# Storing a bias tile partition-major, clearing a dispatch buffer only in the general path, and moving 18 column-sum matmuls, in an FFT + MoE + FFN kernel

## The chip, the cores and the metric

The kernel runs on one core of a Trainium2 chip. The metric is the device time of one execution in microseconds, as the median of several runs. Before the change it is 990.84 us (3 runs, 988.04 to 993.03).

## What is computed

Three steps follow each other; the input x is [8, 3072, 256], and all is float32 at the borders.

```python
X = np.fft.fft(np.fft.fft(x, axis=1), axis=2).real     # 8 batches, 3072 x 256
x = X.reshape(24576, 256)                              # tokens
logits = x @ w_gate                                    # 8 experts
e = argmax(logits); gate = softmax(logits)[e]
# first come, first served: each expert takes its first 768 tokens, by token number
h = relu(disp @ w1[e])                                 # 256 -> 1024
out[token] = gate * (h @ w2[e])                        # 1024 -> 256; zero for tokens without a slot
h = out @ w_in                                         # 256 -> 2048
result = (h * sigmoid(1.702 * h)) @ w_out              # 2048 -> 256, [24576, 256]
```

A token without a slot has a zero row in the result. With 8 experts of 768 slots there are 6,144 slots for 24,576 tokens, so once all experts are full, later tokens are zero rows.

## The kernel before, in words

**Main path and general path.** Because slots are given in token order, the kernel transforms and routes only as many tokens as will fill all experts unless the routing is lopsided: five half batches of 1,536 tokens (`nu` = 5, so `nb` = 3 batches). A flag says at the end whether every expert was filled. If not, `tc.If(more != 0)` at the end of the program enters the general path, which transforms the other batches and repeats the FFNs. With these inputs it isn't entered.

**The transform.** A batch comes as three thirds (row tiles j) of 1 MB, each loaded by SP (`fft_x`, L434) into one of three buffers. `fft_fold` (L444 ff.) adds and subtracts parts on DVE, and the tile is then split into a rounded part (`fhi`, on ACT, L346) and the rest (`flo`, on DVE, L347). For j = 2 the fold also sends two small pieces across partitions by DMA (L468, L469), and ACT copies two more (L470, L471). The first batch takes its thirds in the order 0, 1, 2, the others 0, 2, 1.

The **S stage** (`fft_s`, matmuls of L520) multiplies the folded thirds by cosine and sine tables (`chi`, `clo`) into PSUM tiles `psP`, `psPE`, `psQ` and so on; the third tile ends them. `fft_s_full` (L575 to L592) turns them into `hiP` and `hiQ` in SBUF, on ACT and DVE. The **D stage** (`fft_d`, matmuls of L603 and L607) multiplies these by a second table (`dr`, `dhi`) and gives, in 12 token tiles, the rows of two half batches with their gate logits, copied into `xtok`. The folds of the next batch stand between the D stage's tiles.

**The column sums.** `fft_rows` (L410 ff.) makes one piece for all batches at once: 18 matmuls (L423) into two PSUM tiles `pt` of 8 rows, two conversions on ACT (L425), and a split into `trh` (ACT) and `trl` (DVE). The last matmuls of each batch's S stage into `psQ` take `trh` and `trl` (`sel` picks the batch). It also stores the `bias` tile, 128 x 6 x 8 float32, to `biasd` in DRAM (L414), which only the general path reads. A hook in the S stage of the first batch calls it: `(i, n) == (1, 0)`, that is with the first piece of the second row tile.

**Routing.** For each half batch `choose` and `route` (L647 to L713) find each token's expert on DVE, count with small matmuls, and give each token a slot (`sloti`) or an index out of bounds. POOL then sends the rows to `disp` in DRAM by 12 indirect DMAs per half batch (L713), 128 rows of 260 floats each. `disp` has 6,144 rows; `zero_disp` clears it by eight stores of 768 rows from SP (L263), called at three places: one store behind the small constants' loads, two between loads of x ahead of the first S stage's end, five after it. `self.after(ins, self.last_load)` keeps each behind the load of x issued last.

**The FFNs.** After the third half batch the first blocks of three experts are read back by POOL (`xr`, L841, which waits for the scatters' landing), scaled by the gate (L853) and transposed on PE (L871). The expert FFN goes in blocks of up to three tiles of 128 slots (L898 and L889); the second FFN runs six blocks behind (L943 and L934), and its rows go to `out` by indirect DMA (L965) with the token numbers `ix` (L857). SP stores zero rows to `out` beside it (L271).

**Order of the work.** Each engine, and the SP queue of DMA issues, works through one list in order. The lists come from the order of the calls and from a scheduler; `self.after` pins single pairs.

Of the kernel before, what the change touches and what calls it, by code (L numbers as in the profile page):

```python
# [22 lines left out]
P = 128  # L23
# [15 lines left out]
TINY = float(np.uint32(0x38100000).view(np.float32))   # upper word of 2 ** -126  # L39
XB = 3          # thirds of a batch on chip  # L40
XR = 3          # blocks of rows loaded ahead
SB = 3          # slot tiles per block of the FFN
FIRST = 3       # experts whose first blocks come before all others
ZC = 6          # parts of a half batch's zero rows
LAG = 6         # blocks that the second FFN runs behind the first
D1 = 3          # hidden tiles that the second product of an FFN runs behind the first
# row tiles of the first batch in the order of their loads, and of the others
J0, J1 = (0, 1, 2), (0, 2, 1)
# when a batch's row tiles are folded, during the batch before: "s" at the end of its S stage, "n" with the
# S stage of their own batch, a number with that token tile of the D stage  # L50
FOLD = ((0, "s", 6), (0, 8, 11))
DEXACT = (0, 1)   # batches whose D stage takes float32 operands as they are
SPLIT = (1,)      # batches whose first half is routed in two parts
CHOOSE, ROUTE = 6, 10   # token tiles of the D stage after which the first part is chosen for and routed
EARLY = 9         # token tile of the last D stage after which the first block is turned
LATE = 5          # hidden tile of the first block from which on the last half batch is routed
IN0, IN1 = 5, 7   # hidden tiles with which the next block is gated and turned
LOADS = 4         # hidden tile with which a later block's rows are read
PACE = (1, 1, 1, 2, 1, 1, 1, 2)   # steps of the second FFN's weights with each hidden tile


# s of an octant by row tile: even, odd, half of each
# [7 lines left out]
def consts():  # L70
    """Tables that depend on the shapes alone."""
# [11 lines left out]
    # high and (scaled) low parts of 11 bits each  # L83
    cm = np.stack(blocks, 1).reshape(NJ, P, NS, 2 * HC)
    # the last tile's odd classes: cosines and sines of even s, sines and cosines of odd s
# [3 lines left out]
    # the even classes' second halves mirror their first ones  # L89
# [3 lines left out]
    cm = np.ascontiguousarray(np.stack([ch, cl], 3))           # [NJ, 2, 128, 2, 4 * HC]  # L93
# [11 lines left out]
    cs = np.stack([C, Sf, Sm], 0).astype(np.float32)          # [3, 128, 256]  # L105
    # mirrored logits backwards, 3 of padding, the row, its start again, 3 of padding, logits
# [3 lines left out]
    # [l in tile, l tile, 3, d]  # L110
# [8 lines left out]
    ], 1).astype(np.float16)                                   # [128, 4, 128]  # L119
# [7 lines left out]
    # the mirrored half's last tile starts with its first token  # L127
# [8 lines left out]
def layout(x):  # L136
    """x as the octants of s that the folds pair, d beside -d."""
    s = ROWS
    rows = [s, 768 - s, 1536 - s, 768 + s, 3072 - s, 2304 + s, 1536 + s, 2304 - s]
    pos = np.arange(128)  # L140
    neg = (256 - pos) % 256
    neg[0] = 128
    p2, n2 = neg.copy(), pos.copy()
    p2[0], n2[0] = 0, 128
    xo = np.empty((B, NJ, P, 8, 2, P), np.float32)
    for i, r in enumerate(rows):
        v = x[:, r, :].reshape(B, NJ, P, D)
        xo[:, :, :, i, 0] = v[..., pos if i < 4 else p2]
        xo[:, :, :, i, 1] = v[..., neg if i < 4 else n2]
    er = x[:, [0, 768, 1536, 2304], :]  # L150
    xe = np.stack([er[..., pos], er[..., neg]], 2)             # [B, 4, 2, 128]
    xed = np.ascontiguousarray(xe.transpose(3, 0, 1, 2))       # [128, B, 4, 2]
    xeb = np.ascontiguousarray(xe[..., 0])                     # [B, 4, 2]
    # columns d = 0 and 128 of all batches: [p, j, half, octant, b]
    xt = np.ascontiguousarray(xo[..., 0].transpose(2, 1, 4, 3, 0))
    return xo, xed, xeb.reshape(B, 8), xt


def at(ap, i):
    """Entry i of the first axis, i a number or a register's value."""  # L160
# [6 lines left out]
class K:  # L167
    def __init__(self, ctx, tc, cap, x, xed, xeb, xt, cm, dc, dct, tri, sel, sm, wg, w1, w2, wi, wo, out):
        self.ctx, self.tc, self.nc = ctx, tc, tc.nc
        self.cap = cap  # L170
        self.capt = -(-cap // P)                  # slot tiles per expert
# [10 lines left out]
    # ---------------------------------------------------------------- setup  # L182
    def setup(self):
# [16 lines left out]
        self.base0 = c0.tile([P, E], F32, name="base0")  # L200
# [11 lines left out]
    def tokens(self, n, extra=None):  # L212
        """Room for the rows of n half batches, used in turn."""
# [7 lines left out]
    def scratch(self, *shape):  # L221
        """A part of that room, until the rows need it."""
# [7 lines left out]
    def small_consts(self):  # L230
# [3 lines left out]
        # the next slot of each expert, at first that where its slots start  # L234
# [5 lines left out]
        nc.gpsimd.tensor_copy(out=self.base0, in_=self.start)  # L240

    def check_full(self, n):
        """Multiplies the flag by: every expert has n tokens or more."""
# [7 lines left out]
    def after(self, ins, first):  # L251
        """Keeps ins behind first, if any, on their queue."""
# [5 lines left out]
    def zero_disp(self, es):  # L258
        nc = self.nc
        for e in es:  # L260
            n = self.capt
            v = self.disp[e * n * P : (e + 1) * n * P].rearrange("(p n) w -> p n w", n=n)
            ins = nc.sync.dma_start(out=v, in_=self.zt[:, None, :].to_broadcast([P, n, ROW]))  # L263
            self.after(ins, self.last_load)

    def zero_out(self, h, i):
        """Rows of a part of half a batch."""
# [5 lines left out]
    # ---------------------------------------------------------------- FFT  # L273
    def fft_consts_alloc(self):
# [6 lines left out]
        # signs of the last tile's even and odd s: cosines and sines, high and low  # L281
# [7 lines left out]
    def fft_consts(self, j, low):  # L289
        """Tables of a row tile: the even classes' columns m as stored and, with the sign of s, from the end."""  # L290
# [26 lines left out]
    def fft_dconsts(self):  # L317
        nc = self.nc
        fc = self.fc
        # D stage tables with the gate's columns  # L320
# [9 lines left out]
    def fft_dtables(self):  # L330
        """The D stage's tables, the gate's columns from their product."""
# [17 lines left out]
    def fft_prelude(self):  # L349
        """Edge rows of all batches, and the even classes of column d = 128 (less d = 0)."""  # L350
# [4 lines left out]
        # sums and differences of d and -d  # L355
# [5 lines left out]
        bias = fc.tile([P, 6, B], F32, name="bias")   # P0, P2, P odd, Q odd, the same with signs, 0  # L361
# [11 lines left out]
        self.biasd = self.dram.tile([B, P, 6], F32, name=f"biasd{self.runs}")  # L373
        self.bias = bias
        self.runs += 1
        # column 128: even classes
# [15 lines left out]
        # row 0 changes sign last in the third class  # L392
# [17 lines left out]
    def fft_rows(self):  # L410
        """The even classes of column d = 128, all batches."""
        nc, fc, fx = self.nc, self.fc, self.fx
        hi, lo, bb = self.pre
        nc.sync.dma_start(out=self.biasd.rearrange("b p i -> p i b"), in_=self.bias)  # L414
# [15 lines left out]
    def fft_x(self, b, j):  # L430
        """A third of a batch."""
# [8 lines left out]
    def fft_fold(self, x, j):  # L440
        """Folds a third of a batch: stationary operands of the S stage."""
# [7 lines left out]
        # x: ee1 ee2 v1 v2 | u1 u2 w1 w2 | P0 Q2 P2 Q0  # L449
# [6 lines left out]
        # column 0 of v carries the cosine transform of d = 128 (odd k)  # L456
# [5 lines left out]
        if j < 2:  # L462
            # v1 v2 u1 u2 | P0 Q2 P2 Q0
            src = x[:, 2:14].rearrange("p (g q) d -> p g q d", q=6)[:, :, 0:4]
        else:
            # P0 Q2 P2 Q0 | v2 v1 and u1 u2 of even s, v1 v2 and u2 u1 of odd s, one below the other
# [11 lines left out]
    def terms(self, half, j):  # L478
        """(chunk, [(data, table)]): even classes, sums over even and over odd s of the odd classes."""
# [9 lines left out]
    def fft_s_begin(self, b):  # L489
        """The S stage, transposed: cosine and sine halves [d', k]. Row 0 of the sine half: d = 128."""  # L490
# [33 lines left out]
    def fft_s_end(self, bias, b=None):  # L524
        """High and low parts of the halves."""
# [12 lines left out]
        # classes 1 and 3 (from its end) as sum and difference  # L538
# [29 lines left out]
    def fft_s_full(self, bias):  # L568
        """The halves as they are."""
# [26 lines left out]
    def fft_row(self, PQ, k0, n, name):  # L596
        """Token rows k0 to k0 + n - 1, in the D stage's columns."""
# [14 lines left out]
    def fft_d(self, PQ, xs, hook=lambda t: None):  # L612
        """Token rows of the first half of a batch and those of the second, with their logits.

        Row S - k is row k backwards. The second half's tiles are in falling order, and so are their
        rows; in place of token S the last tile starts with token S / 2."""
# [13 lines left out]
    # ---------------------------------------------------------------- routing  # L630
    def rt(self, name, n, e=1, dt=F32, swap=False, bufs=1):
        """A tile for n tiles of tokens, or [expert, tile] of them."""
# [5 lines left out]
    def choose(self, xt):  # L638
        """Experts of some tiles of tokens."""
# [9 lines left out]
        # the first of equal maxima  # L649
# [322 lines left out]
def kernel(ctx, tc, cap, x, xed, xeb, xt, cm, dc, dct, tri, sel, sm, wg, w1, w2, wi, wo, out):  # L972
# [56 lines left out]
    def route_next(late=False):  # L1029
# [5 lines left out]
        if u + 1 == nu // 2 * 2:  # L1035
            nc.vector.tensor_copy(out=k.base0, in_=k.base)
# [272 lines left out]
```

## Time and profile before

| what | value |
|---|---|
| median of 3 runs | 990.84 us (988.04 to 993.03) |
| span of the profiled execution | 1001.3 us |
| PE busy | 922.4 us, 92% |
| DVE busy | 592.0 us, 59% |
| ACT busy | 513.4 us, 51% |
| POOL busy | 210.2 us, 21% |
| DMA | 96.71 MB in 78,118 packets, 12,633 of them under 512 bytes |

The profiled execution gives no other time than its span, which is 10.5 us above the median of the runs. PE is TensorE's matmuls, PEld its weight loads, which overlap; DVE is VectorE, ACT ScalarE, POOL GpSimd, and SP (SPq) the queue from which most DMAs are issued. A share of the whole span is a mean over stages with different limits. The granted clock is TensorE's, as a share of full speed. A line number is that of the listing above.

### The profile page before, as it was taken

To read this page: it belongs to the slowest core of one execution; us is meant where nothing else is said; L and a number is where in the kernel's file an instruction comes from. 1 tells how busy PE (TensorE), PEld (TensorE's weight loads), DVE (VectorE), ACT (ScalarE), POOL (GpSimd) and SP (SyncE) were. 2 spreads that over 40 slices of the span, in tenths; PEclk is the share of its full clock that TensorE was granted. 3 is DMA by queue.
4 is the path that set the end of the run, shared out by engine and by line. 5 is a ranking of instruction groups with operands and counts; after the bars stand their busy time and mean duration, and the time that the engine had idled before them with its cause. 6 is when DMAs were issued, how large, how long until landed. Compare 5 with 4: busy or idle time off the path is not lost. (4 is left out here: it accounts for less than half of the span.)

```text
span 1001.3 us, 15819 instructions
## 1 busy us (share of the span) xinstructions
PE 922.4 (92%) x5920; PEld 898.5 (90%) x5920; DVE 592.0 (59%) x1175; ACT 513.4 (51%) x1064; POOL 210.2 (21%) x236
## 2 busy tenths in 40 slices
PE   3779287899989999999999999999999999999995
PEld 2558286889989999999999999999999999999995
DVE  7369185898898456545553555555535555555552
ACT  5546063665675446444553555555535554555452
POOL 4006653755556101010101010101010110111011
PEclk9979698999999999999999999999999999999998
DMA  9996357797781106200530020201000000000000
GB/s 342 34 272 212 138 171 250 249 319 230 251 267 53 33 1 202 83 32 2 173 112 33 1 84 18 78 23 59 1 16 1 17 16 1 17 17 17 1 18 19
DMA packets 78118, 96.71 MB, mean 97 GB/s; under 512 B 12633, under 2 KB 67130, under 8 KB 76880
## 3 DMA queue, kind: packets, MB, share of 16 engines
q1 hardware_dynamic: 71056, 76.53, 26.4%
q0 software_dynamic: 6976, 19.09, 5.5%
q8 instruction: 48, 0.79, 0.3%
q14 instruction: 38, 0.31, 0.1%
HBM read 50.93 MB, written 45.86 MB: 97 GB/s over the span
## 5 line engine op out<-in xcount | busy, mean ns | idle before, releaser
L948 DVE TENSOR_TENSOR sg<-ph,sg 128x384 f32<-128x384 f32 x256 | 142.6, 557 | 116.0 <-ACT sg L947 112.6
L952 DVE TENSOR_TENSOR gl<-sg,gh 128x384 fp32r<-128x384 f32 x256 | 146.1, 571 | 107.9 <-ACT gh L951 105.5
L951 ACT CAST gh<-sg 128x384 fp32r<-128x384 f32 x256 | 131.1, 512 | 121.7 <-DVE sg L948 121.7
L947 ACT ACTIVATE sg<-ph 128x384 f32<-128x384 f32 x256 | 125.8, 491 | 108.0 <-PE ph L943 103.7
L965 POOL DMA_INDIRECT out<-orow,ix x48 | 47.1, 980 | 569.0 <-ACT orow L964 559.3
L904 DVE SCALAR_TENSOR_TENSOR hl<-ph,hh 128x384 fp32r<-128x384 f32 x128 | 70.9, 554 | 92.1 <-ACT hh L903 78.3
L903 ACT ACTIVATE hh<-ph 128x384 fp32r<-128x384 f32 x128 | 63.0, 494 | 90.7 <-PE ph L898 85.5
L889 PE MATMUL py<-hh,w2h 128*128 128x384 f32 x256 | 88.2, 345 | 3.0 <-ACT hh L903 1.9
L889 PE MATMUL py<-hl,w2h 128*128 128x384 f32 x256 | 87.1, 340 | 1.1 <-DVE hl L904 1.0
L898 PE MATMUL ph<-xhi,w1l 128*128 128x384 f32 x256 | 85.9, 336 | 1.7 <-issue 1.7
L889 PE MATMUL py<-hh,w2l 128*128 128x384 f32 x256 | 86.4, 337 | 0.0
L898 PE MATMUL ph<-xhi,w1h 128*128 128x384 f32 x256 | 86.0, 336 | 0.4 <-issue 0.4
L898 PE MATMUL ph<-xlo,w1h 128*128 128x384 f32 x256 | 85.8, 336 | 0.4 <-issue 0.4
L713 POOL DMA_INDIRECT disp<-xtok,sloti x48 | 53.8, 1120 | 66.3 <-DMA x<-in_x 38.2
L889 PEld LDWEIGHTS py<-hh,w2h 128*128 128x128 f32 x256 | 48.7, 190 | 4.1 <-ACT hh L903 2.4
L347 DVE TENSOR_TENSOR w2l<-wraw,w2h 128x512 fp32r<-128x512 f32 x44 | 42.0, 961 | 15.9 <-ACT w2h L346 15.3
L889 PEld LDWEIGHTS py<-hl,w2h 128*128 128x128 f32 x256 | 48.6, 190 | 3.2 <-DVE hl L904 2.5
L898 PEld LDWEIGHTS ph<-xlo,w1h 128*128 128x128 f32 x256 | 48.2, 189 | 1.4 <-issue 1.2
L898 PEld LDWEIGHTS ph<-xhi,w1h 128*128 128x128 f32 x256 | 48.2, 188 | 1.2 <-issue 1.2
L889 PEld LDWEIGHTS py<-hh,w2l 128*128 128x128 f32 x256 | 48.7, 190 | 0.0
L898 PEld LDWEIGHTS ph<-xhi,w1l 128*128 128x128 f32 x256 | 48.2, 188 | 0.5 <-issue 0.5
L347 DVE TENSOR_TENSOR w1l<-wraw,w1h 128x512 fp32r<-128x512 f32 x44 | 31.8, 722 | 2.8 <-ACT w1h L346 1.9
(380 smaller groups left out, 2697.0 us busy)
## 6 DMA issues: line engine op xcount, KB each, us to landing
out<-zt SPq DMA_DIRECT2D x96, 256.0 KB
wraw<-in_w SPq DMA_DIRECT2D x88, 256.0 KB
x<-in_x SPq DMA_DIRECT2D x9, 1024.0 KB
disp<-zt SPq DMA_DIRECT2D x8, 780.0 KB
xr<-disp POOLq DMA_DIRECT2D x16, 390.0 KB
wraw<-in_wi SPq DMA_DIRECT2D x8, 512.0 KB
wraw<-in_wo SPq DMA_DIRECT2D x8, 512.0 KB
cr<-in_cm SPq DMA_DIRECT2D x6, 388.0 KB
```

Source lines behind the costliest of these rows:

```text
L347: return h, nc.vector.tensor_tensor(out=lo, in0=src, in1=hi.bitcast(F32), op=ALU.subtract)
L713: ins = nc.gpsimd.indirect_dma_start(out=self.disp, out_offset=bass.IndirectOffsetOnAxis(ap=sloti[:, i : i + 1], axis=0), in_=xt[:, i, 0:R ...
L889: nc.tensor.matmul(py[a][:, :n], lhsT=w2[f // 2][v][:, f % 2, a * P : (a + 1) * P], rhs=(hh, hl)[u][:, :n], start=(f == 0 and k == 0), sto ...
L898: nc.tensor.matmul(ph[:, :n], lhsT=w1[f // 2][v][:, a, (f % 2) * P : (f % 2 + 1) * P], rhs=(xh, xl)[u][:, a, :n], start=(k == 0), stop=(k ...
L903: self.last_a = nc.scalar.activation(out=hh[:, :n], in_=ph[:, :n], func=AF.Relu)
L904: self.last_v = nc.vector.scalar_tensor_tensor(out=hl[:, :n], in0=ph[:, :n], scalar=0.0, in1=hh[:, :n].bitcast(F32), op0=ALU.max, op1=ALU. ...
L947: nc.scalar.activation(out=sg[:, :n], in_=ph[:, :n], func=AF.Sigmoid, scale=1.702)
L948: nc.vector.tensor_tensor(out=sg[:, :n], in0=ph[:, :n], in1=sg[:, :n], op=ALU.mult)
L951: nc.scalar.copy(out=gh[:, :n], in_=sg[:, :n])
L952: nc.vector.tensor_tensor(out=gl[:, :n], in0=sg[:, :n], in1=gh[:, :n].bitcast(F32), op=ALU.subtract)
L965: ins = nc.gpsimd.indirect_dma_start(out=out, out_offset=bass.IndirectOffsetOnAxis(ap=xr[:, i : i + 1], axis=0), in_=orow, in_offset=None, ...
```

## The change

1. The `bias` tile is stored as it lies in SBUF: `biasd` is [P, 6, B] in place of [B, P, 6]. The general path reads a batch's part from it by a strided load.
2. `zero_disp` loses its three calls in the main path and clears all of `disp` at the start of the general path. That path then begins anew, from batch 0 and from `self.start`, and clears `out` too; so the copy `base0` of the counts goes. Rows of `disp` that no token reached now hold what the memory held, so `ix` is cut off at an index out of bounds.
3. The hook for `fft_rows` moves from `(1, 0)` to `(2, 0)`: from the first piece of the second row tile to the first piece of the third.

The changed file has three lines less ahead of these places, so L414 there is L411, and so on.

```diff
-        self.biasd = self.dram.tile([B, P, 6], F32, name=f"biasd{self.runs}")
+        self.biasd = self.dram.tile([P, 6, B], F32, name=f"biasd{self.runs}")
...
-        nc.sync.dma_start(out=self.biasd.rearrange("b p i -> p i b"), in_=self.bias)
+        nc.sync.dma_start(out=self.biasd, in_=self.bias)
...
-        nc.gpsimd.tensor_copy(out=self.base0, in_=self.start)
...
-    def zero_disp(self, es):
+    def zero_disp(self):
         nc = self.nc
-        for e in es:
+        for e in range(E):
             n = self.capt
             v = self.disp[e * n * P : (e + 1) * n * P].rearrange("(p n) w -> p n w", n=n)
-            ins = nc.sync.dma_start(out=v, in_=self.zt[:, None, :].to_broadcast([P, n, ROW]))
-            self.after(ins, self.last_load)
+            nc.sync.dma_start(out=v, in_=self.zt[:, None, :].to_broadcast([P, n, ROW]))
...
-        ins = nc.vector.tensor_copy(out=ix[:, :ns], in_=xr.bitcast(I32)[:, :ns, 257])
+        ins = nc.vector.tensor_scalar(out=ix.bitcast(U32)[:, :ns], in0=xr.bitcast(U32)[:, :ns, 257], scalar1=OOB,
+                                      scalar2=None, op0=ALU.min)
...
     k.small_consts()
-    k.zero_disp(range(1))
     fold(0, J0[2])
...
-        if u + 1 == nu // 2 * 2:
-            nc.vector.tensor_copy(out=k.base0, in_=k.base)
...
-                if b == 0 and (i, n) == (1, 0):
+                if b == 0 and (i, n) == (2, 0):
                     k.fft_rows()
...
             xload()
-            k.zero_disp(range(1, 3))
             xload()
...
         if b == 0:
-            k.zero_disp(range(3, E))
             xload()
...
     with tc.If(more != 0):
-        nb = nu // 2
...
+        k.zero_disp()
+        for h in range(2 * B):
+            for i in range(ZC):
+                k.zero_out(h, i)
+        nc.sync.dma_start(out=k.smt, in_=k.sm)
...
-                nc.vector.tensor_copy(out=k.base, in_=k.base0)
-                with tc.For_i(nb, B, 1) as b:
+            nc.vector.tensor_copy(out=k.base, in_=k.start)
+            with tc.For_i(0, B, 1) as b:
...
-                    nc.sync.dma_start(out=bt, in_=at(k.biasd, b))
+                nc.sync.dma_start(out=bt[:, :, None], in_=k.biasd[:, :, bass.ds(b, 1)])
```

How the lists move is shown at three places. The first is the SP queue from the load of the table `tri` to the loads of x for the second batch. L263 are the stores that zero `disp`, L414 the bias store, L434 the loads of x. Before:

```order
L233 DMA tri<-in_tri 128x512
L263 DMA disp<-zt 768x1x260
L468 DMA x<-x 64x2x128
L469 DMA x<-x 64x2x128
L494 DMA sf<-in_sel 8x128
L414 DMA biasd_193<-bias 768x8x1
L434 DMA x<-in_x 128x2048
L263 DMA disp<-zt 768x1x260 x2
L434 DMA x<-in_x 128x2048
L263 DMA disp<-zt 768x1x260
L468 DMA x<-x 64x2x128
L469 DMA x<-x 64x2x128
```

and now (three lines less, so L411 is the bias store and L431 a load of x):

```order
L232 DMA tri<-in_tri 128x512
L465 DMA x<-x 64x2x128
L466 DMA x<-x 64x2x128
L491 DMA sf<-in_sel 8x128
L411 DMA biasd_192<-bias 128x48
L431 DMA x<-in_x 128x2048 x2
L491 DMA sf<-in_sel 8x128 x2
L465 DMA x<-x 64x2x128
L466 DMA x<-x 64x2x128
L431 DMA x<-in_x 128x2048 x3
```

The zeroing stores are gone, and loads of x stand next to each other behind the bias store.

The second place is ACT, at the end of the first batch's S stage: L425 are the two conversions of the column sums, `fhi` of L346 is the third row tile's rounded part. Before:

```order
L471 COPY x<-x 64x256
L425 ACTIVATE xtokx<-pt_301,bb 8x386
L425 ACTIVATE xtokx<-pt_312,bb 8x384
L346 CAST trh<-xtokx 8x772
L346 CAST fhi<-x 128x1024
L496 CAST sel_267<-sf 8x128
L592 ACTIVATE hiP<-psP_269,bias 128x386
```

and now, with L422 the conversions and L343 the cast:

```order
L468 COPY x<-x 64x256
L343 CAST fhi<-x 128x1024
L493 CAST sel_264<-sf 8x128
L589 ACTIVATE hiP<-psP_266,bias 128x386
L589 ACTIVATE hiP<-psP_270,bias 128x384
L335 COPY dr<-pw 128x2x8
L336 COPY dr<-pw 128x2x8
L343 CAST dhi<-dr 128x560
L422 ACTIVATE xtokx<-pt_337,bb 8x386
L422 ACTIVATE xtokx<-pt_348,bb 8x384
L577 ACTIVATE eb<-psPE,bias 128x384
L343 CAST trh<-xtokx 8x772
```

The conversions stood ahead of the third tile's cast; they now follow `hiP`'s two rows, and the cast of `trh` is the last of these.

The third is DVE at the same place: `trl` is the rest of the column sums, L444 the first add of a fold (of the next batch's thirds), L581 to L587 make `hiP` and `hiQ`. Before:

```order
L347 TENSOR_TENSOR trl<-xtokx,trh 8x772
L347 TENSOR_TENSOR flo<-x,fhi 128x1024
L581 TENSOR_TENSOR hiP<-eb,psPO 128x384
L583 TENSOR_TENSOR hiP<-eb,psPO 128x384
L444 TENSOR_TENSOR x<-x 128x1024
L347 TENSOR_TENSOR dlo<-dr,dhi 128x560
L581 TENSOR_TENSOR hiQ<-eb,psQO 128x384
L587 SCALAR_TENSOR_TENSOR hiQ<-psQO,ngs,t_411 128x384
```

and now (L441 is the first add of a fold):

```order
L344 TENSOR_TENSOR flo<-x,fhi 128x1024
L441 TENSOR_TENSOR x<-x 128x1024
L344 TENSOR_TENSOR dlo<-dr,dhi 128x560
L443 TENSOR_TENSOR x<-x 128x512
L444 TENSOR_TENSOR x<-x 128x512
L448 TENSOR_TENSOR x<-x 128x512
L449 TENSOR_TENSOR x<-x 128x512
L441 TENSOR_TENSOR x<-x 128x1024
L344 TENSOR_TENSOR trl<-xtokx,trh 8x772
L578 TENSOR_TENSOR hiP<-eb,psPO 128x384
L580 TENSOR_TENSOR hiP<-eb,psPO 128x384
L578 TENSOR_TENSOR hiQ<-eb,psQO 128x384
```

One fold's start stood ahead of `hiQ`; now two (a whole first fold but for its split, and the first add of the second) stand ahead of `trl`, `hiP` and `hiQ`.

## Rows read from the trace of the kernel before

**Rows 1.** Part 1 of the page: the span.
```profile
span 1001.3 us, 15819 instructions
```

**Rows 2.** Busy us by stretch: length, PE, PEld, DVE, ACT, POOL; clock, DMA, GB/s.
```profile
100.00:125.00 25.00, 6.96 (x30) 5.82 (x28) 4.37 (x26) 1.23 (x4) 17.09 (x20) 0.62 0.39 138
...
200.00:225.00 25.00, 23.81 (x134) 22.47 (x134) 24.51 (x41) 15.77 (x32) 14.27 (x12) 1.00 0.98 319
...
700.00:800.00 100.00, 100.00 (x683) 100.00 (x682) 51.38 (x95) 49.48 (x103) 5.83 (x6) 1.00 0.02 9
```

**Rows 3.** Who waited for whom, 0 to 235 us: total, times, longest.
```profile
POOL disp L713 <- DMA x<-in_x: 38.2, 1, 38.2
...
DVE x L444 <- DMA x<-in_x: 23.7, 3, 15.0
```

**Rows 4.** Timeline of the SP queue: start, duration of the issue, what.
```profile
26.42 0.60 SPq L414 DMA_DIRECT2D biasd<-bias  x1
27.12 9.19 SPq L434 DMA_DIRECT2D x<-in_x  x1
```

**Rows 5.** Busy time by stretch, 32 to 36 us.
```profile
32.00:36.00 4.00, 4.00 (x23) 3.55 (x21) 2.17 (x2) 2.26 (x4) 0.00 (x0) 1.00 1.92 1
```

**Rows 6.** Timeline of DVE: start, duration, what, idle time before and its releaser.
```profile
5.88 1.23 DVE L444 TENSOR_TENSOR x<-x 128x1024 f32<-128x1024 f32 x1 [4.86 <-DMA x<-in_x]
...
53.34 1.22 DVE L444 TENSOR_TENSOR x<-x 128x1024 f32<-128x1024 f32 x1 [15.04 <-DMA x<-in_x]
...
63.86 1.23 DVE L444 TENSOR_TENSOR x<-x 128x1024 f32<-128x1024 f32 x1 [3.80 <-DMA x<-in_x]
...
76.07 0.17 DVE L699 SCALAR_TENSOR_TENSOR sloti<-over,pos 128x12 int32<-128x12 f32 x1
```

**Rows 7.** Timeline of PE, at the changes of stage.
```profile
24.20 0.49 PE L423 MATMUL pt<-chi,thi 128*8 128x386 f32 x1 [4.25 <-ACT thi L346]
...
41.38 0.63 PE L603 MATMUL pe<-dr,hiP 128*1 128x280 f32 x2
...
56.74 2.23 PE L603 MATMUL pd<-dr,hiQ 128*128 128x280 f32 x4 [13.12 <-DVE hiQ L587]
...
69.36 0.55 PE L520 MATMUL psP<-chi,fhi 128*128 128x386 f32 x1
...
97.97 0.54 PE L520 MATMUL psP<-chi,fhi 128*128 128x386 f32 x1
...
135.83 0.96 PE L607 MATMUL pd<-dhi,hiP 128*128 128x280 f32 x5
...
145.72 0.95 PE L871 MATMUL pt<-smt,xr 128*128 128x128 f32 x6
...
148.06 0.34 PE L898 MATMUL ph<-xhi,w1h 128*128 128x384 f32 x1
```

**Rows 8.** Timeline of POOL: scatters and the first reads of blocks.
```profile
80.59 1.23 POOL L713 DMA_INDIRECT disp<-xtok,sloti  x1 [38.21 <-DMA x<-in_x]
...
97.16 1.12 POOL L713 DMA_INDIRECT disp<-xtok,sloti  x1 [0.23 <-issue]
...
120.78 0.97 POOL L713 DMA_INDIRECT disp<-xtok,sloti  x1 [0.23 <-issue]
...
138.54 2.34 POOL L841 DMA_DIRECT2D xr<-disp  x3 [1.83 <-DMA disp<-xtok,sloti]
```

**Rows 9.** Busy time of line 423 alone, 19 to 32 us.
```profile
19.00:32.00 13.00, 4.68 (x18) 1.80 (x18) 0.87 0.72 158
```

**Rows 10.** Timeline of ACT: two rows of the first batch, one of the third.
```profile
29.44 0.40 ACT L471 COPY x<-x 64x256 f32<-64x256 f32 x1
...
32.45 1.04 ACT L346 CAST fhi<-x 128x1024 fp32r<-128x1024 f32 x1
...
124.77 0.58 ACT L535 ACTIVATE eb<-psPE,bias 128x384 f32<-128x384 f32 x1 [20.99 <-remote]
```

**Rows 11.** Busy time of line 603 alone, 85 to 98 us.
```profile
85.00:98.00 13.00, 12.42 (x52) 9.21 (x52) 1.00 0.36 124
```

More of the change, by code (lines that the diff above doesn't have):

```diff
@@ L199, in setup @@
         self.base = c0.tile([P, E], F32, name="base")
-        self.base0 = c0.tile([P, E], F32, name="base0")
         self.flag = c0.tile([P, 1], F32, name="flag")
@@ L1236 @@
     with tc.If(more != 0):
-        nb = nu // 2
-        if nb < B:
-            with ExitStack() as c1:
-                k.rp = c1.enter_context(tc.tile_pool(name="rp2", bufs=1))
-                k.fxt = c1.enter_context(tc.tile_pool(name="fxt2", bufs=1))
-                k.tokens(2)
-                k.fq = c1.enter_context(tc.tile_pool(name="fq2", bufs=1))
-                k.fc = c1.enter_context(tc.tile_pool(name="fc2", bufs=1))
-                k.fx = c1.enter_context(tc.tile_pool(name="fx2", bufs=2))
-                k.fft_consts_alloc()
-                for j in range(NJ):
-                    k.fft_consts(j, nc.vector)
-                k.fft_dconsts()
-                k.fft_dtables()
-                k.fft_prelude()
-                k.fft_rows()
-                nc.vector.tensor_copy(out=k.base, in_=k.base0)
-                with tc.For_i(nb, B, 1) as b:
-                    data = {j: k.fft_load(b, j) for j in J1}
-                    bt = k.fx.tile([P, 6], F32, name="bt", tag="bt", bufs=1)
-                    nc.sync.dma_start(out=bt, in_=at(k.biasd, b))
-                    k.fft_s_begin(b)
-                    for j in J1:
-                        k.fft_s(b, j, data[j])
-                    PQ = k.fft_s_end(bt)
-                    xs = [next(k.slot) for _ in range(2)]
-                    k.fft_d(PQ, xs)
-                    for mir, xt in enumerate(xs):
-                        k.route(xt, mir, None)
@@ new lines @@
+        k.zero_disp()
[3 more added lines that the diff above has]
+        nc.sync.dma_start(out=k.smt, in_=k.sm)
+        with ExitStack() as c1:
+            k.rp = c1.enter_context(tc.tile_pool(name="rp2", bufs=1))
+            k.fxt = c1.enter_context(tc.tile_pool(name="fxt2", bufs=1))
+            k.tokens(2)
+            k.fq = c1.enter_context(tc.tile_pool(name="fq2", bufs=1))
+            k.fc = c1.enter_context(tc.tile_pool(name="fc2", bufs=1))
+            k.fx = c1.enter_context(tc.tile_pool(name="fx2", bufs=2))
+            k.fft_consts_alloc()
+            for j in range(NJ):
+                k.fft_consts(j, nc.vector)
+            k.fft_dconsts()
+            k.fft_dtables()
+            k.fft_prelude()
+            k.fft_rows()
+            nc.vector.tensor_copy(out=k.base, in_=k.start)
+            with tc.For_i(0, B, 1) as b:
+                data = {j: k.fft_load(b, j) for j in J1}
+                bt = k.fx.tile([P, 6], F32, name="bt", tag="bt", bufs=1)
+                nc.sync.dma_start(out=bt[:, :, None], in_=k.biasd[:, :, bass.ds(b, 1)])
+                k.fft_s_begin(b)
+                for j in J1:
+                    k.fft_s(b, j, data[j])
+                PQ = k.fft_s_end(bt)
+                xs = [next(k.slot) for _ in range(2)]
+                k.fft_d(PQ, xs)
+                for mir, xt in enumerate(xs):
+                    k.route(xt, mir, None)
```

## The prediction

> **What bounds the kernel now.** I began with the span and then cut it into stretches [rows 1, 2]. From 700 to 800 us PE is busy for 100 of 100 us at full clock; from 100 to 125 it is busy for 6.96 of 25. So the second half of the program is bound by PE's work, which the change doesn't touch, and anything to be won lies before the expert FFN starts, at 148.06 us in this trace. Next I read who waited for whom in the first 235 us [rows 3]. Two waits on DMA stand out: POOL's first row scatter waited 38.2 us, and DVE's folds waited 23.7 us for loads of x.
>
> The SP queue and the stretch around the store show where the DMA time goes [rows 4, 5]. The store of the bias tile is issued at 26.42. From 32 to 36 us the DMA engines are busy (a share over 1 means overlapping packets) and move 1 GB/s. This is 24 KB in 6,144 elements of 4 bytes. The load of x issued behind it at 27.12 is used by DVE only at 53.34, and the next load at 63.86 [rows 6]. DVE works in order, so the last part of the first batch's S stage (hiQ) stands behind that fold, and PE waits 13.12 us for it, starting the D stage at 56.74 [rows 7]. Among these loads SP issues the eight stores of 780 KB that zero the dispatch buffer. The first scatter, whose slots DVE had finished by 76.24 [rows 6], starts at 80.59 [rows 8]. Its row names a load of x as the releaser; what it really needs is the zeroing, which is behind those loads in the same queue.
>
> From there the **scatter queue on POOL** matters most. 30 scatters run from 80.59 to 121.75, the last six of the third half batch come next, and the reads of the first expert blocks, which need all of these landed, are issued at 138.54 [rows 8]. PE multiplies the first block at 148.06, 9.5 us later [rows 7].
>
> **The change, part by part.**
>
> *The bias store.* Partition-major it is 128 runs of 192 bytes in place of 6,144 of 4. The trace has no such store. Its cost lies between nothing and that of the 24 KB as it stands, some 25 us of blocked DMA; the nearest rows are loads of x of 1 MB, of which the first, issued at the program's start among others, is used at 5.88 [rows 6]. I take below 1 us, hidden beside ACT's and PE's work.
>
> *The zeroing.* Eight stores of 780 KB leave the path, and with them the scatter's wait. Nothing else reads them: with every expert full all rows are overwritten. The loads of x come earlier on SP by what they were queued behind. The load of 27.12 should be usable some 5 us later, at 32, and the next (its buffer is free when the third fold is done, an estimate of 32 from the cast's start [rows 10]) at 37 to 38.
>
> *The 18 column-sum matmuls.* They take 4.68 us of PE, at a mean clock of 0.87 in that stretch [rows 9]. They leave the middle of the second row tile, where PE waited 4.25 us ahead of them [rows 7], and now stand in the third. ACT's conversions of their result stood between 29.84, when the copies of L471 end, and the cast at 32.45 [rows 10]; that cast now follows the copies, 2.6 us earlier. From the cast to the first D matmul (41.38 [rows 7]) PE needed 8.9 us. So 29.84 + 8.9 + 4.7 = 43.5. On DVE the correction term trl, hiP and hiQ come last, behind two folds' starts, and PE's two rows with trl stand behind hiP. I add 2 us for that: hiQ is ready and the D stage starts at **45.5**, not 56.74. The PE stall in front of the moved matmuls is worth nothing by itself, because the third tile's operands are not there earlier; it turns into idle time before the third tile.
>
> *From there to the scatters.* The D stage took 12.6 us, to 69.36, at a slower clock after the stall. The next batch's D stage at full clock has 12.42 us of PE [rows 11]; of the first batch's, some 1.6 us stand ahead of hiQ (41.38 on), so 10.8 are left. The second S stage starts at 56.3. DVE had the slots 6.9 us after that start (69.36 to 76.24). The first scatter goes at **63.2 instead of 80.59: 17.4 us earlier.**
>
> *On the scatter queue.* 30 scatters took 41.2 us, which gives 104.4; six more at 1.29 us (the pace of the last 19) end at 112.4, and after the 1.83 us wait for their landing the reads go out at 114.2. Meanwhile PE's own work would be done sooner: S and D of the second batch (69.36 to 97.97, 28.6, so to 84.9), the third S stage (97.97 to 135.83, of which some 20 are idle time; an S stage of 28.6 - 12.4 = 16.2 and some waits are left, say 16.5), and the 9.9 us from the D stage's start to the transposes of the first block (135.83 to 145.72 [rows 7]): 111.3. The block's rows arrive 7.2 us after their read, at 121.4. So PE gets **a new wait of some 10 us** there, and the scatter queue decides.
>
> *The rest.* The vector copy of 128 by 3 indices, once per block, becomes a minimum of as many elements, and two copies of 8 columns go: nothing, beside a DVE that is idle half of the time from 700 to 800 us [rows 2]. The general path isn't entered.
>
> **The sum.** Against the profiled execution: the FFN starts at 114.2 + 9.5 = 123.7 instead of 148.06, so 24.4 us of its 1001.3 us span. But 7 us of these belong to the stall that ended at 124.8, where ACT stood for 20.99 us and the row names no instruction as its releaser ("remote") [rows 10]. Without it the scatters of 121.75 would have run on and the reads gone out at 131.6, and the same change is worth 131.6 - 114.2 = 17.4. The span is already 10.5 us above the runs' median of 990.84, so I take it that the runs don't have that stall: 990.8 - 17.4 = **973.4 us**.
>
> Beside DVE's folds the scatters were slower. The 11 from 80.59 to 97.16 took 1.51 us each, the 19 from there to 121.75 1.29 [rows 8]. The page *SBUF — State Buffer* of the Trainium skill (sections "SBUF: two separate sides" and "A bandwidth-pool intuition that's wrong") speaks against moving scatters beside folds: some DVE instructions, those with two SBUF inputs among them, and GpSimd exclude each other from a shared port for the whole instruction, and a transfer issued from GpSimd grew from 620 to 3100 ns beside a DVE copy. By that page an estimate for 24 scatters moved beside folds would be some 24 x 2.5 us later, and no gain would be left. The trace agrees in kind, not in size: 0.2 us a scatter.
>
> **The rivals.**
>
> 1. *The long stall goes too.* If the runs do have the stall of 21 us, it goes with the congestion, and the reads move by the full 138.54 - 114.2. For: nothing in the program waits there. Against: the runs lie below the span. Time: 990.8 - 24.4 = 966.4.
> 2. *The scatter queue gives part back.* All 24 scatters of the first batch run beside folds, at 1.51 us or more. That is 24 x 1.51 = 36.2 instead of 31.2 us, and if the slots also come 1.5 us later, 6.5 less gain: 980. For: the first 11 rows. Against: the folds take DVE no longer than before, so no more than about as many scatters meet them. The page's rule, at the size that the rows bear out, is this rival.
> 3. *The FFN swallows it.* If the first blocks were bound by weight loads, an earlier start would only wait: from 200 to 225 us DMA is at 0.98 [rows 2]. PE is busy for 23.81 us of that stretch, so PE and not DMA is full there. Time: 989.
> 4. *Slower.* In the new order DVE starts the fold of the load issued second ahead of trl, hiP and hiQ; before, only one load stood ahead of hiQ. If that load comes no earlier than now (63.86), for instance because the store stays slow, the D stage starts some 5.4 us later (3.4 from the fold's start as today, 53.34 to 56.74, and an estimate of 2 for trl and hiP), at 69.3 in place of 56.74. The first scatter would follow 12.6 + 6.9 us later at 88.8, 8.2 us behind today's: 999. It decides against the kernel if the load lands after 55.6. With nothing large left in the DMA queues at 27 us I see no reason for more than 38.
>
> **How the numbers follow.** A difference under 0.5% (5 us) is no difference for this measurement; the three runs shown lie 5 us apart. My forecast, 968 to 978, has 0.55; rival 1, with what more may go of unexplained stalls (960 to 968), 0.20; rival 2 (978 to 985) 0.14; rival 3 0.08; rival 4 0.03. Faster by over 0.5%: 0.55 + 0.20 + 0.14 and a part of rival 3, 0.91; same 0.06; slower 0.03. Forecast and rivals 1 and 2 hold nearly 9 in 10, so the range is 960 to 984.
>
> **What would show it.** Right: no stretch near 32 us with busy DMA and no bytes; the D stage starting at 44 to 47; the first scatter at 61 to 65, now waiting for DVE's slots and not for DMA; the reads of the first blocks at 112 to 117; PE idle ahead of the first block's transposes for the rows; the FFN at 121 to 126, and from there the same time to the end. Wrong: a first scatter later than 70, scatters above 1.6 us each, or a new PE wait for weights after the FFN's start.

## The result, and the profile after

| | median, us | lowest to highest | runs |
|---|---|---|---|
| before | 991.34 | 988.04 to 993.03 | 4 |
| changed | 980.87 | 978.42 to 981.18 | 4 |

The ratio is 0.9886, with a 95% interval of 0.9863 to 0.9909: 10.5 us, or 1.1%, less. The forecast was 973.4 us with a range of 960 to 984. So the sign and the range hold, and the size is some 60% of the 17.4 us that were forecast. The time lies outside the forecast's own band of 968 to 978 us and in that of rival 2, 978 to 985.

The span of the profiled execution, against [rows 1] (whose trace has the stall of [rows 10], so that the two spans don't give the gain):

```profile
span 979.4 us, 15819 instructions
```

Who waited for whom from 0 to 235 us, against [rows 3] (total, times, longest, in us):

```profile
PE pt L870 <- DVE xr L850: 21.7, 4, 14.0
POOL disp L710 <- DVE pp L686: 20.2, 1, 20.2
...
PE psP L517 <- ACT fhi L343: 18.0, 2, 12.9
...
DVE x L441 <- DMA x<-in_x: 9.0, 2, 5.0
```

DVE's waits for x fell from 23.7 to 9.0 us. POOL's first scatter waits for DVE's slots, no longer for DMA. PE has a wait of 14.0 us for the gated rows of the first block, which the shown trace of before doesn't have.

PE at the changes of stage, against [rows 7] (start, duration, what, idle time before and its releaser):

```profile
31.07 0.69 PE L517 MATMUL psP<-chi,fhi 128*128 128x386 f32 x1 [5.08 <-ACT fhi L343]
...
37.10 0.52 PE L420 MATMUL pt<-chi,thi 128*8 128x386 f32 x1
...
45.78 0.63 PE L600 MATMUL pe<-dr,hiP 128*1 128x280 f32 x2
...
48.97 1.11 PE L600 MATMUL pd<-dr,hiQ 128*128 128x280 f32 x4
...
59.13 0.55 PE L517 MATMUL psP<-chi,fhi 128*128 128x386 f32 x1
...
126.55 0.66 PE L870 MATMUL pt<-smt,xr 128*128 128x128 f32 x2 [14.04 <-DVE xr L850]
...
130.55 0.34 PE L897 MATMUL ph<-xhi,w1h 128*128 128x384 f32 x1
```

The 13.12 us wait ahead of the D stage is gone. In its place PE stands for 5.08 us ahead of the third row tile, at 31.07, and the column sums come at 37.10. The busy times by stretch show what follows from that idle time (length; PE, PEld, DVE, ACT, POOL; granted clock, DMA share, GB/s):

```profile
26.00:31.00 5.00, 0.00 (x0) 0.00 (x0) 3.29 (x9) 4.96 (x10) 0.54 (x1) 0.99 0.74 218
31.00:35.00 4.00, 3.85 (x12) 2.91 (x12) 2.36 (x2) 1.86 (x4) 0.00 (x0) 0.50 0.50 137
35.00:41.00 6.00, 6.00 (x23) 3.53 (x23) 3.17 (x6) 1.48 (x4) 0.00 (x0) 0.50 0.26 106
```

The granted clock is 1.00 from 19 to 26 us; behind the gap it is 0.50, the lower of the two levels, for ten microseconds.

POOL's scatters and the reads, against [rows 8]:

```profile
66.97 1.43 POOL L710 DMA_INDIRECT disp<-xtok,sloti  x1 [20.19 <-DVE pp L686]
...
119.67 0.97 POOL L710 DMA_INDIRECT disp<-xtok,sloti  x1 [0.23 <-issue]
122.48 2.33 POOL L838 DMA_DIRECT2D xr<-disp  x3 [1.84 <-DMA disp<-xtok,sloti]
```

36 scatters start over 52.7 us, 1.51 us apart, with no gap over 0.31 us between two. The queue on POOL decides when the first blocks are read.

### The profile page after: what moved, and what is told of

Same layout as the page of the kernel before. It is cut to its first block, busy times and chain, and to the rows that moved or that the text cites. A ratio compares the mean times of both kernels' runs of the same rounds, so it can differ in the third digit from the quotient of the medians.

```text
span 979.4 us, 15819 instructions
## 1 busy us (share of the span) xinstructions
PE 918.0 (94%) x5920; PEld 897.6 (92%) x5920; DVE 590.4 (60%) x1174; ACT 514.7 (53%) x1064; POOL 211.9 (22%) x235
## 5 line engine op out<-in xcount | busy, mean ns | idle before, releaser
L902 ACT ACTIVATE hh<-ph 128x384 fp32r<-128x384 f32 x128 | 63.0, 493 | 76.3 <-PE ph L897 75.2
L710 POOL DMA_INDIRECT disp<-xtok,sloti x48 | 57.2, 1192 | 40.8 <-DVE pp L686 20.2
L870 PE MATMUL pt<-smt,xr 128*128 128x128 f32 x96 | 15.1, 293 | 21.7 <-DVE xr L850 21.7
```

The lines of the kernel that those rows point to most:

```text
L710: ins = nc.gpsimd.indirect_dma_start(out=self.disp, out_offset=bass.IndirectOffsetOnAxis(ap=sloti[:, i : i + 1], axis=0), in_=xt[:, i, 0:R ...
L870: nc.tensor.transpose(pt[:, i * P : (i + 1) * P], xr[:, i, a * P : (a + 1) * P], self.ident)
L902: self.last_a = nc.scalar.activation(out=hh[:, :n], in_=ph[:, :n], func=AF.Relu)
```

## The experiments

**The kernel before, once more** (e1). No edit.

> The kernel before once more, for a second profile. Theory (the 21 us idle time of ACT at 104 to 125 us belongs to that one profiled execution): it is gone, the first blocks are read at about 131.6 us, the first FFN matmul starts at 141 and the span is 989 to 992. Rival (it belongs to the kernel): it is there again, the FFN starts at 148 and the span is about 1001.

Its span is 987.9 us, its median 992.06 beside 991.88 (ratio 1.0002, 0.9989 to 1.0014).

```profile
137.01 0.45 PE L871 MATMUL pt<-smt,xr 128*128 128x128 f32 x1 [12.45 <-DVE xr L853]
```

The reads go out at 132.94 and the FFN starts at 141.80: the theory holds, but for a span some 1 us below it, and 141.1 was the working's figure without the stall. So the kernel before, too, had a PE wait of 12.45 us for the first block. The start of its FFN was bound by POOL's queue already; the shown trace hid this behind its stall.

**One part undone at a time** (e2 to e4).

```diff
# e2
-                if b == 0 and (i, n) == (2, 0):
+                if b == 0 and (i, n) == (1, 0):
# e3: the three calls of zero_disp back, each store behind the last load of x
+    k.zero_disp(range(1), True)
...
+            k.zero_disp(range(1, 3), True)
...
+            k.zero_disp(range(3, E), True)
# e4, with biasd as [B, P, 6] again
-        nc.sync.dma_start(out=self.biasd, in_=self.bias)
+        nc.sync.dma_start(out=self.biasd.rearrange("b p i -> p i b"), in_=self.bias)
```

> The changed kernel with the column-sum matmuls back in the first piece of the second row tile. Theory (behind the move, PE waits 5.08 us ahead of the third row tile and then works 10 us at the lower clock, which costs more than the 4.25 us wait it removes): hiQ's part of the D stage starts 5 to 6 us earlier than 48.97, the first scatter at 61 to 62 instead of 66.97, the reads at 117, and the time is 975 to 977, below the changed kernel's 980.9. Rival (the move is worth what the wait ahead of the matmuls was): first scatter at 70 to 71, time 984 to 986.

> The changed kernel with the eight zeroing stores back at their three places. Theory (the bias store was what held the loads and the zeroing up; behind a quick store the zeroing is through before DVE has the slots): the first scatter at 67 to 70 and the time 981 to 984. Rival (the 6.2 MB of zeroing hold up the loads and the scatters by themselves): first scatter at 76 or later, 988 to 991.

> The changed kernel with the bias store in its old order of 4-byte elements. Theory (this store alone holds the loads behind it up to 52 us or so, and two folds now stand ahead of trl, hiP and hiQ on DVE): the D stage's hiQ part starts at 58 to 63, the first scatter at 77 to 81, and the time is 988 to 995, as slow as before or slower. Rival (the zeroing was what the loads waited for): first scatter at 67 to 70, time 981 to 984.

And **the store alone** (e9): e2 and e3 together.

> The changed kernel with the zeroing and the column-sum matmuls both back in their old places, so that the bias store is the only part of the change left in the main path. Theory (the store alone is worth the whole gain, and the move of the matmuls takes some of it back): the D stage's hiQ part at 47 to 48, the first scatter at 64 to 67, time 973 to 977, below the whole change's 980.9. Rival (the parts need each other): 981 to 988.

| run | store partition-major | zeroing gone | sums moved | us | ratio to before (95%) |
|---|---|---|---|---|---|
| e1 | no | no | no | 992.06 | 1.0002 (0.9989 to 1.0014) |
| e9 | yes | no | no | 975.18 | 0.9826 (0.9809 to 0.9842) |
| e2 | yes | yes | no | 974.93 | 0.9840 (0.9824 to 0.9857) |
| e3 | yes | no | yes | 977.55 | 0.9866 (0.9849 to 0.9884) |
| change | yes | yes | yes | 980.87 | 0.9886 (0.9863 to 0.9909) |
| e4 | no | yes | yes | 995.80 | 1.0040 (1.0022 to 1.0057) |

The theories hold on the sign of every edit, with misses in place and size. e3 came out below the 981 to 984 expected. In e4 hiQ's part started at 63.96 instead of 58 to 63, the scatters at 83.43 instead of 77 to 81, and the time is just above 988 to 995. In e2 hiQ's part came at 47.56, 1.4 us ahead of the change and not 5 to 6, and the first scatter at 64.88, not at 61 to 62; in e9 hiQ's part came at 43.60, ahead of the 47 to 48 expected.

```profile
47.56 1.11 PE L600 MATMUL pd<-dr,hiQ 128*128 128x280 f32 x4
```

```profile
43.60 1.11 PE L602 MATMUL pd<-dr,hiQ 128*128 128x280 f32 x4
```

The first row is e2's, the second e9's. PE's order around them is the same; the granted clock isn't (last section).

The store alone brings 1.7%, more than the whole change. The zeroing's removal beside it brings nothing that can be told (e9 and e2). The move costs 0.4 to 0.5% with or without the zeroing (e9 to e3, e2 to the change, each beside its own runs of before; the intervals of both pairs don't overlap). In e2 the reads go out at 118.93 (3.6 us ahead of the change), the FFN starts at 127.54 (3.0 ahead), and the wait ahead of the fourth block's transposes is 3.5 us instead of 6.7: together the 6 us between the two kernels. Why that second wait differs isn't shown. Without the new store the other two parts make the kernel slower, by rival 4's mechanism: two folds now stand ahead of trl, hiP and hiQ on DVE.

```profile
59.17 1.00 PE L517 MATMUL psQ<-trl,sel 8*128 8x386 f32 x2 [13.47 <-DVE trl L344]
...
63.96 2.07 PE L600 MATMUL pd<-dr,hiQ 128*128 128x280 f32 x4
```

These are PE's rows of e4; in [rows 7] the part with hiQ started at 56.74.

What the zeroing costs shows in e9's POOL row:

```profile
65.45 1.23 POOL L712 DMA_INDIRECT disp<-xtok,sloti  x1 [22.92 <-DMA x<-in_x]
```

DVE has the slots at 60.1, and the scatter starts 5.3 us later; in e2, without the zeroing, it starts 1.0 us after the slots (63.9). The row names a load; what the program makes it wait for is the zeroing, whose last four stores are issued from 47.98 on. The scatters then go 1.41 us apart instead of e2's 1.46, and the FFN starts at 126.28, e2's at 127.54. But e9's slots came 3.8 us ahead of e2's at the higher clock, so these two traces don't show the zeroing alone. That a scatter queue which starts later meets fewer folds, and so gives part of the wait back, is argued and not shown; that folds slow the scatters is the next experiment.

**Scatters beside folds** (e5). The changed kernel without the adds and subtractions of the third batch's folds (7 for each of three thirds, 21 in all; the expectation says 18).

```diff
-                data[j] = k.fft_fold(xq.pop((b, j)), j)
+                data[j] = k.fft_fold(xq.pop((b, j)), j, b < 2)   # False: no adds
...
```

> The changed kernel without the 18 adds and subtractions of the third batch's folds on DVE (that part of the transform is left out; loads, splits and all else stay). Theory (a scatter that meets a DVE instruction with two SBUF inputs ends 0.92 us after that instruction): the first 14 scatters, 1.60 us apart in the changed kernel, come to 1.35 to 1.45, and the reads of the first blocks to 118 to 120 from 122.48. Rival (the loads of x share the DMA queues with the scatters and slow them): they stay at 1.55 to 1.65, since the loads are still there.

From the first scatter to the fifteenth the changed kernel took 23.65 us, 1.69 each (the 1.60 of the expectation divided by one too many); e5 took 19.99, 1.43 each. The loads of x are the same in both. So the adds are the cause of this difference, and the rival falls. (e5's reads go out at 121.64 and not at 118 to 120; 5.23 us of idle time in its queue at 98.9 belong to the stall told of below.) In the changed kernel's own rows the collision can be read singly, DVE first:

```profile
79.23 0.67 DVE L443 TENSOR_TENSOR x<-x 128x512 f32<-128x512 f32 x1
...
81.03 0.67 DVE L444 TENSOR_TENSOR x<-x 128x512 f32<-128x512 f32 x1
```

```profile
79.25 1.50 POOL L710 DMA_INDIRECT disp<-xtok,sloti  x1 [0.30 <-ACT xtokx L622]
81.06 1.50 POOL L710 DMA_INDIRECT disp<-xtok,sloti  x1 [0.30 <-ACT xtokx L622]
82.86 0.97 POOL L710 DMA_INDIRECT disp<-xtok,sloti  x1 [0.30 <-ACT xtok L620]
```

The first scatter starts 0.02 us after the add and ends at 80.75, 0.85 after the add's end at 79.90; the second likewise, 0.86 after 81.70. Of the 10 scatters up to 140 us that start under an add or split of a fold, six end 0.85 or 0.86 us after it, and the mean of the ten is 1.61 us; the other 34 have 1.04, and 28 of them 0.97 to 0.99. The Trainium skill states in *SBUF — State Buffer*, "SBUF: two separate sides", that a DVE instruction with two SBUF inputs and a GpSimd instruction that reads SBUF hold a shared port for a whole instruction, whichever starts first locking the other out. The trace agrees with a lock of this kind. The size differs: the page's growth of a transfer from 620 to 3100 ns is beside a DVE copy, here a scatter of 0.97 us grows to 1.97 at most among these 44, as it waits for the rest of the add or split (0.67 to 1.23 us) that it met.

e5 to e8 were run together on a chip where the kernel before took 999.55 us, and each of their profiles has a stretch of 10 to 25 us between 90 and 125 us in which PE, ACT and DVE stand with "issue" or "remote" as the releaser. So rows behind 90 us are not compared with those of the other runs, nor e5's time (989.92 us) with theirs, and the edits of e6, e7 and, with the hook of e6, e8 were run again.

**The column sums in the gap** (e6, e10).

```diff
-                if b == 0 and (i, n) == (2, 0):
+                if b == 0 and (i, n) == (1, 5):
```

> The changed kernel with the column-sum matmuls ahead of the last piece of the second row tile. Theory (they then fill the idle time ahead of the third row tile, and PE keeps the higher clock): hiQ's part of the D stage starts at 42 to 45, the first scatter at 60 to 63, the reads at 114 to 117, the time is 970 to 975. Rival (the conversions on ACT then hold up the third row tile, or PE still waits long enough to lose the clock): first scatter at 65 or later, 976 to 981.

> Once more the changed kernel with the column-sum matmuls ahead of the last piece of the second row tile, whose first scatter started at 62.8. Theory (each microsecond by which the scatter queue starts earlier comes out at the end): reads at 115 to 116, FFN at 123 to 126, 970 to 974. Rival (later waits take it back): 975 or more.

hiQ's part starts at 45.57 and 45.47, the first scatter at 62.81 and 62.72, 4 us ahead of the change; in e10 the reads follow at 117.04, a little behind the theory, and the FFN at 125.11. e6 measured 988.57 beside its 999.55; e10 gives 975.40 us, 0.9833 (0.9813 to 0.9852). The first scatter is 2 us ahead of e2's, and the FFN 2.4, and the time is the same: the wait ahead of the fourth block's transposes is 6.7 us again, where e2 has 3.5. So e10's rival holds. e6's theory had PE keep the higher clock; it did not, and hiQ's part missed the 42 to 45 expected. The granted clock is 0.50 from 31 to 36 us in e6 and from 31 to 35 in e10, about half as long as in the change.

**Earlier reads** (e7, e11; then e8, e12). The first three blocks need 384 rows of an expert only, which 3,840 tokens give here as well as 4,608, so the reads can go out after 30 scatters.

```diff
# e7, e11, on e2
-        if t0 + xt.shape[1] < HT:
-            return
-        if u == ua:
+        if u == ua and not xrs:
             k.check_full(min(na, cap))
...
# e8, e12 also (e12 with the hook at (1, 5))
-LATE = 5
+LATE = 0
...
+    if units:
+        send_step()
     ys = []
```

> The column-sum matmuls back in the second row tile, and the first three blocks read after 30 scatters instead of 36, once the first half of the third half batch is sent (3,840 tokens; the check that all experts have 384 rows is made there). Theory (the scatter queue alone sets the start of the FFN): reads at 110 to 112 instead of 118.9, FFN at 119 to 121 instead of 127.5, time 967 to 970. Rival (the scatters that were left make the fourth block late): the wait at the fourth block's transposes grows by what the start gained, and the time stays at 973 to 976.

> Once more the matmuls in the second row tile with reads after 30 scatters. Theory (the scatter queue sets the start of the FFN): reads at 109 to 110, FFN at 118 to 121, time 966 to 969. Rival (the scatters left over make a later block wait by as much): a wait of 8 us or more at the transposes after 160, time 973 to 976.

> As the run with early reads, and the last half batch is routed ahead of the first block and sent with its hidden tiles from the first on, so that POOL has no gap between the fourth and the fifth half batch's scatters. Theory: all 60 scatters end by 165 instead of 185, the wait at the fourth block's transposes (3.5 to 7 us) goes, time 963 to 967. Rival (its routing on DVE stands ahead of the first block's hidden rows and makes PE wait there instead): no better than the run with early reads.

> The column-sum matmuls ahead of the last piece of the second row tile, early reads, and the last half batch routed ahead of the first block. Theory: reads at 107 to 109, FFN at 116 to 119, no wait over 4 us at the transposes of later blocks, 962 to 966. Rival (routing on DVE ahead of the first block's hidden rows makes PE wait there): a PE wait of 2 us or more between 115 and 145 that the run with early reads lacks, and no better than that run.

In e11 the reads go out at 108.52 and the FFN starts at 117.35, 10.2 us ahead of e2 and a little ahead of the theory. The time is 976.83 us, 0.9843 (0.9810 to 0.9877): nothing gained. Who waited in e11 from 112 to 185 us shows where it went:

```profile
ACT w64m L792 <- POOL wi0l L811: 10.6, 1, 10.6
...
PE py L888 <- ACT hh L902: 8.8, 1, 8.8
```

```profile
165.23 1.26 POOL L811 TENSOR_TENSOR wi0l<-w64m,w64t 128x512 fp32r<-128x512 f32 x1
```

POOL also converts the second FFN's weights (L809 to L811), and these stand in its list between scatters of the last half batch, which start at 155.23. ACT's list has the next piece of weights (L792) ahead of the FFN's hidden rows (hh, L902), and it waits until POOL is done at 166.49. PE stands for 8.8 us. Half the rival, then: the gain is lost to the scatters left over, but by way of POOL's weights and ACT, not of a late block. e7 gave 988.77 and e8 993.28 beside 999.55 us, no better than e6. e12 starts the FFN at 121.77 behind a wait of 2.89 us for DVE's routing, as its rival says, then has the same wait for hh (8.7 us), and gives 976.35, 0.9850 (0.9820 to 0.9879). The theory of e11 and of e12 falls.

So the best versions are e9 and e2, with e10 beside them, some 975 us, and beyond them no edit of the start came out at the end.

The start of the FFN is not what the time follows. From the first transposes of the fourth block to the end it is 791.0 to 792.4 us in all nine profiles without the stall: the transposes start at 180.77 in e2, 180.97 in e10, 182.12 in e11, 187.45 in the change and 196.27 in e1. From the FFN's start to them it is 53.2 us in e2, 55.9 in e10, 56.9 in the change and 64.8 in e11. What releases them in all of these, e12 apart, is in the last section: DVE's scaling, held up by POOL's adds on the weights.

## Why the prediction was right, and where its sum was wrong

| step | forecast | measured |
|---|---|---|
| kernel before, FFN's start without the stall | 131.6 + 9.5 = 141.1 | 141.80 (e1) |
| third tile's cast on ACT | 29.84 | 29.97 |
| hiQ's part of the D stage | 45.5 | 48.97 |
| second S stage | 56.3 | 59.13 |
| first scatter | 63.2 | 66.97 |
| PE's own work ahead of the first block | 111.3 | 112.5 (126.55 - 14.04) |
| reads of the first blocks | 114.2 | 122.48 |
| FFN's start | 123.7 | 130.55 |

The signs for the D stage (44 to 47, with hiQ's part), the first scatter (61 to 65), the reads (112 to 117) and the FFN (121 to 126) were all missed, by 2.0 to 5.5 us; the others came true: the DMA engines move 217 GB/s from 32 to 36 us, the first scatter waits for slots, and PE stands idle for the first block's rows. Of the signs of being wrong, scatters above 1.6 us each came true up to the fifteenth (1.69), not for all 36 (1.51).

**The store.** That its cost would be hidden was right: the new one lands 1.5 us after its issue, and nothing waits for it. The old one was the cause of the folds' wait: behind the new one the next folds start at 32.19 and 40.98 without a wait for their loads. Undoing it alone costs 15 us (e4), and it alone gives more than the whole change does (e9).

**The zeroing.** The first scatter's wait was rightly read as the zeroing's. That its removal would be worth something was wrong: with the new store it holds the first scatter up by some 4 us (e9), and nothing of that can be told at the end.

**The stall.** That the runs don't have it was right, as far as a second profile and the medians show (e1), and it carried 7 us of the choice between 17.4 and 24.4.

**The moved matmuls** are the step that failed. "It turns into idle time before the third tile" came true, 5.08 us of it, but I priced PE's work behind it at the 8.9 us that it had taken at the full clock. After the idle time PE ran at 0.50 for 10 us, and the first D matmul came at 45.78 instead of 43.5. And from there to hiQ's part it took 3.2 us instead of the 2 that I had added for trl, hiP and hiQ: the 18 matmuls run from 37.10 to 42.3, mostly at the lower clock, and trl, which hiQ needs, comes behind them. Together these make 3.5 us at hiQ and 3.8 at the first scatter. Without the move (e2) the time is 974.93, which is nearer to the forecast than the change itself. How much of the 3.5 us is the move's doing alone is open: in e2 the clock fell too, later (0.50 from 40 to 44 us), and hiQ's part came 1.4 us earlier; in e9, at the higher clock from 28 us on, 5.4 us earlier.

**The scatter queue** was mis-sized. 41.2 us for 30 and 1.29 for each of six more gave 51.0 us from the first scatter to the reads; it took 55.5. I had put scatters beside folds into rival 2, at 1.51 us each; the 36 took 1.51 apart. Rival 2, slots 1.5 us later included, gave 980, and this is nearest to what happened: the same lock (e5), with the slots later still. That its figure came so near is in part luck: the 41.2 us for 30 scatters hold 11 at 1.51 us already, so the first 24 stand in the sum with some 33.4 us and not 31.2, and rival 2 would have been 977.7. The estimate of 24 times 2.5 us took a copy's figure for adds; the ten scatters that met an add or split took 1.61 us on the mean where a free one takes 0.97.

Sum: the reads came 8.3 us late (3.8 + 4.5), the step from reads to FFN took 8.07 instead of 9.5, so the FFN started 6.85 late. 17.4 less 6.85 is 10.5 us, the measured gain, but so close a fit is luck. In the traces the FFN starts 11.25 us ahead of e1's, and 2.75 of these are lost behind it: 846.1 us from there to the end in e1 (987.9 less 141.80), 848.9 after the change. The spans of the two differ by 8.5 us; e1's profiled execution (989.54 us) was 2.5 below its median. The rival of the weights (rival 3) isn't seen in the changed kernel; a neighbour of it appears once the FFN starts 10 us earlier still (e11).

## What to carry to other kernels

A store of 4-byte elements costs little where it is issued and much where its queue's next load is used: look at what stands behind it, and mend it alone before anything else. Work moved out of a wait leaves the wait behind, and TensorE may go on at the lower clock after it; fill the gap or leave the work there. Where one queue (here POOL's scatters, locked out by DVE's adds) feeds all that follows, an earlier start is worth only what that queue, and the next wait behind it, let through: look for the point from which the time to the end is the same in all runs (here the fourth block's transposes), and ask what each edit does to that.

## What was not expected

- e2 and e11 have the same order up to 60 us, yet hiQ's part starts at 47.56 in e2 and at 43.62 in e11. From 40 to 44 us PE is busy without a gap in both, at these clocks (e2 first):

```profile
40.00:44.00 4.00, 4.00 (x12) 3.05 (x11) 1.18 (x2) 2.95 (x6) 0.00 (x0) 0.50 0.04 13
```

```profile
40.00:44.00 4.00, 4.00 (x18) 2.49 (x18) 2.74 (x5) 2.45 (x5) 0.19 (x1) 1.00 0.03 7
```

  From 32 to 40 us PE was busy for 7.31 of 8 us in e2 and 7.67 in e11. Of the other runs with this order up to there, e7 and e8 fell like e2 (hiQ's part at 47.52 and 47.50); e9, with the zeroing, kept the clock like e11. Those that kept it ran on one chip, the others on two more. Why the clock fell in some stays open.
- DVE is locked out too. In the changed kernel the three scalings of 128 x 256 for the fourth block took 4.72 us together while POOL ran its adds on the weights; those for the third block took 0.92. PE's transposes wait for them (DVE, POOL and PE):

```profile
184.26 4.72 DVE L850 TENSOR_SCALAR xr<-xr 128x256 f32<-128x256 f32 x3
```

```profile
185.97 1.26 POOL L810 TENSOR_TENSOR w64m<-w64m,wi1h 128x512 f32<-128x512 f32 x1
```

```profile
187.45 0.47 PE L870 MATMUL pt<-smt,xr 128*128 128x128 f32 x1 [6.66 <-DVE xr L850]
```

  The first transpose starts 0.22 us after that add ends (187.23). It is so in eight of the nine profiles without the stall, the kernel before among them (e1: 4.72 us, too, and 0.22), so it isn't an effect of the change. No run takes these adds from POOL.
- The stall of [rows 10] is no fault of one trace: all profiles of e5 to e8 have one at the same place of the program, and none of the other nine profiles taken after the first has, while POOL's scatters go on at 1.28 us through it, but for 5.23 us in e5. What holds the other engines there isn't in the records.
